# Reshaped loads of x, a class without mirrored rows, and constant tables moved between engines, in a Fourier-mixing + MLP-Mixer kernel

## The chip, the cores and the metric

The kernel runs on one core of one Trainium2 chip. The metric is the device time of one execution, in microseconds (us), lower is better. "Span" is the time of the one execution that was profiled, from its first to its last instruction; it is 1.7 to 3.0 us shorter than the time measured for the same execution.

Engine names in the profile: PE is TensorE's matrix products, PEld its weight loads, DVE is VectorE, ACT is ScalarE, POOL is GpSimd, SP is SyncE. L315 is line 315 of that kernel's source; lines shift by a few between kernels.

## The reference

```python
x: (8, 3008, 256)      # batch, sequence, features
x = np.fft.fft(np.fft.fft(x, axis=1), axis=2).real          # Fourier mixing
h = np.maximum(x.transpose(0, 2, 1) @ w_tok1, 0) @ w_tok2   # token MLP: 3008 -> 256 -> 3008
u = x + h.transpose(0, 2, 1)
out = u + np.maximum(u @ w_ch1, 0) @ w_ch2                  # channel MLP: 256 -> 1536 -> 256
```

The sequence length is factored as 3008 = 47 x 64. A real Fourier transform has mirror symmetry, so the kernel needs, beside each row of x, the row mirrored around the middle of the sequence.

## The kernel before

All loads go out through GpSimd's queue. `load_x` brings a batch into two tiles: `xp`, the rows in order, as two copies of 47 partitions, and `xm`, the mirrored rows, as gathers of 94 rows (two gathers of 8 rows of x at a time, and a third gather of one row for the class r = 0, which are the rows whose number is a multiple of 64).

```python
KR = 2 * NQ            # 94
def load_x(b, between=None):
    xp = xin.tile([KR, NR, D], FP16, tag="xp", name="xp")
    xm = xin.tile([KR, NR, D], FP16, tag="xm", name="xm")
    for i in range(2):
        nc.gpsimd.dma_start(
            out=xp[i * NQ:(i + 1) * NQ, :, :],
            in_=dram(x_t, (b * S + 16 * i) * D, [[64 * D, NQ], [1, NR * D]]))
    ...
    xmf = xm[:].rearrange("p t d -> p (t d)")
    for k in range(2):
        gather(xmf[:, 8 * D * k:8 * D * (k + 1)], x8, ix8[0:KR, b, k:k + 1])
    gather(xmf[:, 16 * D:17 * D], x1, ix1[0:KR, b:b + 1])
    return xp, xm
```

Behind batch 0 in the same queue come the weights: w_tok1 in order (`w1p`) and mirrored (`w1m`), w_tok2 (`w2s`), then the channel weights. Meanwhile VectorE and ScalarE build the sine tables: the small tables of the first stage (`cs`, `t1n`, `t1a`, `t1b`), of the feature stage (`td0`, `td1`), and the large third-stage tables (`tp`, `tq`). VectorE works out the reduced angles, ScalarE takes the sine.

Then come the pieces that decide when the steady stage can begin:

```python
def turned(src, sgn):      # transposes on PE, evicted by ScalarE -> tt
    ...
def carried(tts, dst):     # token weights carried through the third stage
    for g2 in range(NG // 2):
        ph = ps_mm("ph")
        for k in range(2):
            ...
            nc.tensor.matmul(o, lhsT=tts[0][:, g, :], rhs=w1p[:, g, :], ...)             # L313
            nc.tensor.matmul(o, lhsT=tts[1][:, g, :], rhs=w1m[:, NG - 1 - g, :], ...)    # L315
        copy(...)
...
tts_p = turned(tp, 1.0)
tts_q = turned(tq, -1.0)
take(fold(0, nc.vector), 4)    # sums and differences of xp and xm -> eo, on VectorE
...
own = front(0)                 # the Fourier stages of batch 0: pz products first
take(own, 4)
carried(tts_p, hp)
take(own, 4)
carried(tts_q, hq)
...                            # rest of front(0), then the channel MLP (mm1, mm2) for all batches
```

`front(b)` starts with products `pz` of `eo` with `t1n`, evicted to `z`. In the program of PE the first four groups of `pz` stand ahead of the carried products (and in its trace they start at 28.8 us, the carried products at 33.7), so these need the turned tables, w1p, w1m, and the `pz` products ahead of them.

## Time and profile before

| before | |
|---|---|
| time, median of the first 3 runs | 698.62 us (697.92 to 698.90) |
| span of the profiled execution | 695.8 us |
| PE busy | 655.8 us (94%) |
| first carried product that needs w1m | 35.5 us |
| first product of the channel MLP (`pc`) | 57.26 us |

The first two lines of the page give the totals:

```profile
span 695.8 us, 12517 instructions
...
PE 655.8 (94%) x5342; PEld 460.3 (66%) x5342; DVE 336.5 (48%) x621; ACT 318.0 (46%) x604; POOL 222.6 (32%) x180
```

Those 94% are an average over a start in which PE is mostly idle and a long stage in which it never is. The windows view shows it. Each line is a stretch of time, its length, then the busy time (and number of instructions) of each engine, the granted clock of PE, the DMA share and GB/s:

```profile
core 0: us, PE busy (x) PEld busy (x) DVE busy (x) ACT busy (x) POOL busy (x), PEclk, DMA share, GB/s
0.00:20.00 20.00, 1.46 (x12) 1.30 (x13) 15.46 (x61) 5.64 (x9) 11.59 (x20) 1.00 0.96 117
20.00:35.00 15.00, 6.42 (x39) 3.55 (x39) 8.96 (x20) 8.59 (x14) 3.83 (x5) 0.77 1.33 182
35.00:50.00 15.00, 11.70 (x97) 9.38 (x97) 7.99 (x14) 9.80 (x17) 6.16 (x5) 0.84 1.06 171
150.00:600.00 450.00, 450.00 (x3735) 317.63 (x3733) 203.92 (x353) 210.46 (x413) 161.83 (x120) 1.00 0.25 55
```

From 150 to 600 us PE is busy in 450.00 of 450 us, so there is no idle time of PE that a faster engine or load could fill. What this change can win lies in the first 60 us. The chain of waits (start, length, what) says what the start is waiting for:

```profile
10.99 0.67 POOL w1p L144
11.66 23.83 DMA w1m<-in_moe_w_tok_dram
...
35.53 0.37 PE ph L315
```

One load, w1m, takes 23.8 us from its issue, and PE's first product with it starts at once when it lands. The DMA view (tiles, queue, kind, number, KB each, median us from issue to landing) shows that everything near the gathers is slow, but not the direct copies of x:

```profile
DMA packets 50583, 44.03 MB, mean 63 GB/s; under 512 B 18144, under 2 KB 47504, under 8 KB 49776
...
xp<-in_x_dram POOLq DMA_DIRECT2D x16, 399.5 KB, 6.2
...
w2s<-in_moe_w_tok_dram POOLq DMA_DIRECT2D x1, 1504.0 KB, 31.0
...
w1m<-in_moe_w_tok_dram POOLq DMA_DIRECT2D x1, 384.0 KB, 23.8
...
xm<-in_x_dram,ix_77 POOLq DMA_INDIRECT x16, 21.2
```

Of the 16 completion events of that w1m, 12 had come by 24.9 us, when the gathers had landed (24.5 and 25.1 us); the other four came at 35.0 to 35.5 us. The Trainium skill ("DMA: Bandwidth & Descriptors", section "Why a DMA increments its semaphore by 16 and not by 1") says that each engine posts its own increment after its own share of the data. Four of sixteen engines were thus late with their share. The completion events of the two gathers of 94 rows ahead show which: of the first gather's 16 events, 14 came by 8.6 us and two only at 23.9 and 24.5; of the second's, 12 came by 9.4 us and four at 24.6 to 25.1. So the rows of the first gather sat on two engines, the second added two more, and the loads behind them came late on just those four.

### The profile page before, as it was taken

The page shows a single profiled execution, that of the slowest core. Times are in us where ns is not written, and L with a number is a line of the kernel's source. Part 1 is how long each engine was busy: PE and PEld are TensorE (multiplying, and loading weights), DVE is VectorE, ACT ScalarE, POOL GpSimd, SP SyncE. Part 2 cuts the span into 40 slices and gives each one's busy share as a digit, 9 for nine tenths or more (in the row PEclk, how much of TensorE's full clock was granted, in tenths as well). Part 3 has the DMA queues.
Part 4 walks back from the last instruction along what each step waited for, and adds up shares of the span by engine and source line. Part 5 has one row for each costly group of instructions (what it writes and reads, how often), then busy time and mean ns, then how long its engine had stood idle before and what let it go on. Part 6 is the DMA issues. An engine that isn't in the chain of part 4 may idle for free.

```text
span 695.8 us, 12517 instructions
## 1 busy us (share of the span) xinstructions
PE 655.8 (94%) x5342; PEld 460.3 (66%) x5342; DVE 336.5 (48%) x621; ACT 318.0 (46%) x604; POOL 222.6 (32%) x180
## 2 busy tenths in 40 slices
PE   0479999999999999999999999999999999999996
PEld 0265667666766677666776677667776677666665
DVE  8547863653445433654345533554335533453341
ACT  2556553445443555344543554344453454434342
POOL 6230209909902393208810294206700000000000
PEclk9889999999999999999999999999999999999999
DMA  8992341441432126212431116311111211211222
GB/s 111 178 174 41 77 78 33 78 90 47 80 78 61 28 53 117 50 31 58 82 75 46 43 31 116 72 31 40 50 31 31 57 33 31 54 38 35 54 61 57
DMA packets 50583, 44.03 MB, mean 63 GB/s; under 512 B 18144, under 2 KB 47504, under 8 KB 49776
## 3 DMA queue, kind: packets, MB, share of 16 engines
q0 software_dynamic: 24928, 18.60, 17.6%
q1 hardware_dynamic: 25600, 24.65, 13.9%
q8 instruction: 41, 0.67, 0.4%
q14 instruction: 14, 0.11, 0.1%
HBM read 37.06 MB, written 24.64 MB: 89 GB/s over the span
## 4 chain that ended last, share of the span: by engine, by line
PE 91%; DMA 3%; DVE 3%; ACT 1%; POOL 1%; issue 1%; ACTq 0%; DVEq 0%; POOLq 0%
PE po L481 36%; PE pc L460 34%; PE pu L436 6%; DMA w1m<-in_moe_w_tok_dram 3%; PE py L419 2%; PE py L421 2%; PE po L484 2%; PE po L486 2%; PE pw L389 1%; PE pz L366 1%; PE pw L390 1%; ACT w2p L324 1%; PE ph L315 0%; DVE ut L444 0%; PE ph L313 0%
## 5 line engine op out<-in xcount | busy, mean ns | idle before, releaser
L460 PE MATMUL pc<-ut,wc1p 128*128 128x512 f16 x576 | 140.7, 379 | 2.3 <-DVE c_681 L85 1.2
L460 PE MATMUL pc<-ut,wc1m 128*128 128x512 f16 (+1 forms) x576 | 135.1, 370 | 0.0
L491 ACT ACTIVATE osb<-po 128x512 f32<-128x512 f32 x88 | 52.6, 598 | 113.2 <-PE po L486 113.2
L460 PEld LDWEIGHTS <-wc1m 128*128 128x128 f16 x576 | 54.0, 98 | 51.6 <-issue 0.4
L460 PEld LDWEIGHTS <-wc1p 128*128 128x128 f16 x576 | 52.3, 98 | 52.7 <-issue 4.4
L444 DVE TENSOR_TENSOR ut<-pu,yt 128x512 f16<-128x512 f32 (+1 forms) x96 | 61.6, 674 | 52.0 <-PE pu L436 52.0
L347 POOL TENSOR_TENSOR xd<-xp,xm 94x1024 f16<-94x1024 f16 (+1 forms) x24 | 53.7, 2238 | 98.8 <-DMA xm<-in_x_dram,ix_77 98.8
L349 POOL TENSOR_TENSOR eo<-xp 94x512 f16<-94x512 f16 (+1 forms) x24 | 29.1, 1211 | 111.0 <-PE pz L378 109.4
L348 POOL TENSOR_TENSOR xp<-xp,xm 94x1024 f16<-94x1024 f16 (+1 forms) x24 | 53.7, 2237 | 1.9
L436 PE MATMUL pu<-w2p,uu 128*128 128x512 f16 (+1 forms) x192 | 50.1, 375 | 0.0
L486 PE MATMUL po<-anti,ut 128*128 128x128 f16 x192 | 41.8, 218 | 0.0
L484 PE MATMUL po<-ident,ut 128*128 128x128 f16 x192 | 41.7, 217 | 0.0
L324 ACT ACTIVATE w<-pw 128x258 f16<-128x258 f32 x90 | 30.5, 385 | 23.3 <-PE pw L390 23.1
L423 ACT ACTIVATE yt<-py 128x512 f16<-128x512 f32 x48 | 26.6, 597 | 21.1 <-PE py L421 16.7
L322 DVE CAST z<-pz 128x480 f16<-128x480 f32 (+1 forms) x36 | 22.4, 691 | 24.4 <-PE pz L366 15.9
L353 POOL TENSOR_TENSOR eo<-xd 94x508 f16<-94x508 f16 (+1 forms) x24 | 29.0, 1207 | 0.0
L324 ACT ACTIVATE z<-pz 128x480 f16<-128x480 f32 (+1 forms) x28 | 18.3, 670 | 20.1 <-PE pz L366 19.9
L123 POOL DMA_INDIRECT xm<-in_x_dram,ix_77 x16 | 24.3, 1518 | 4.8 <-issue 4.8
L419 PE MATMUL py<-tp,w 128*128 128x128 f16 x192 | 24.7, 219 | 0.7 <-DVE ut L444 0.7
L389 PE MATMUL pw<-td_161,z 128*128 128x258 f16 x96 | 21.8, 274 | 2.9 <-ACT w L324 1.5
L436 PEld LDWEIGHTS <-uu 128*128 128x128 f16 x192 | 16.4, 97 | 9.1 <-issue 0.2
L131 POOL DMA_DIRECT2D xp<-in_x_dram x16 | 9.2, 582 | 39.8 <-DVE eo L351 39.6
(404 smaller groups left out, 1274.5 us busy)
## 6 DMA issues: line engine op xcount, KB each, us to landing
out_dram<-osb SPq DMA_DIRECT2D x88, 256.0 KB, 3.4
xp<-in_x_dram POOLq DMA_DIRECT2D x16, 399.5 KB, 6.2
out_dram<-osb SPq DMA_DIRECT2D x8, 192.0 KB, 3.1
w2s<-in_moe_w_tok_dram POOLq DMA_DIRECT2D x1, 1504.0 KB, 31.0
w1p<-in_moe_w_tok_dram POOLq DMA_DIRECT2D x2, 384.0 KB, 20.5
wc_129<-in_moe_w_ch_dram POOLq DMA_DIRECT2D x1, 768.0 KB, 23.5
w1m<-in_moe_w_tok_dram POOLq DMA_DIRECT2D x1, 384.0 KB, 23.8
wc1p<-in_moe_w_ch_dram POOLq DMA_DIRECT2D x1, 384.0 KB, 19.6
```

What stands on the lines that cost most here:

```text
L324: nc.scalar.activation(out=out_, in_=in_, func=AFT.Copy)
L347: eng.tensor_tensor(out=xd[:, t, :], in0=xp[:, t, :], in1=rv, op=AT.subtract)
L348: eng.tensor_tensor(out=xp[:, t, :], in0=xp[:, t, :], in1=rv, op=AT.add)
L349: eng.tensor_tensor(out=eo[:, t, 1:129], in0=xp[:, t, 1:129], in1=xp[:, t, 255:127:-1], op=AT.add)
L419: nc.tensor.matmul(o, lhsT=w[:, g, h:h + P], rhs=tp[:, g, :], start=True, stop=False)
L436: nc.tensor.matmul(pu[:, 0:n], lhsT=uu[:, th, v, o:o + P], rhs=w2p[:, th, f0:f0 + n], start=(th == 0), stop=(th == 1))
L444: nc.vector.tensor_tensor(out=ut[:, h, f0:f0 + n], in0=pu[:, 0:n], in1=y, op=AT.add)
L460: nc.tensor.matmul(pc[:, 0:n], lhsT=wc[:, h, ct * P:(ct + 1) * P], rhs=ut[:, h, f0:f0 + n], start=(h == 0), stop=(h == 1))
L481: nc.tensor.matmul(po[0:n, o:o + D], lhsT=c1[:, ct, ks * P:ks * P + n], rhs=wc2[:, ct, minus:minus + D], start=(ct == 0), stop=False)
L484: nc.tensor.matmul(po[0:n, o:o + P], lhsT=ut[:, 0, f0:f0 + n], rhs=ident[:], start=False, stop=False)
L486: nc.tensor.matmul(po[0:n, o + P:o + D], lhsT=ut[:, 1, f0:f0 + n], rhs=anti[:], start=False, stop=True)
L491: nc.scalar.activation(out=osb[:, ks - 1:ks + 1, minus:minus + D], in_=src, func=AFT.Copy)
```

## The change

Its intent: spread the loads of x over more DMA engines by giving them piece sizes that divide well; drop the third gather, by treating the class r = 0 without mirrored rows; make the large third-stage tables first on VectorE, and the small tables on GpSimd beside it (so the first loads of the channel weights, which GpSimd issues too, move behind these tables). Its core (full of small moves of code, cut at "..."):

```diff
+KG = 96
...
-    ts(ix8[:], ix8f[:], rowi[:], AT.add)
-    ...                                    # ix1: indices of the third gather
+    ts(ix8[:], ix8f[:], rowi[:], AT.add, 0.0, AT.max)
...
-        xm = xin.tile([KR, NR, D], FP16, tag="xm", name="xm")
+        xm = xin.tile([KG, NR - 1, D], FP16, tag="xm", name="xm")
         for i in range(2):
-            nc.gpsimd.dma_start(out=xp[i * NQ:(i + 1) * NQ, :, :], ...)
+            for q, n in ((0, 32), (32, NQ - 32)):
+                p0 = i * NQ + q
+                nc.gpsimd.dma_start(out=xp[p0:p0 + n, :, :], ...)
...
-            gather(xmf[:, 8 * D * k:8 * D * (k + 1)], x8, ix8[0:KR, b, k:k + 1])
-        gather(xmf[:, 16 * D:17 * D], x1, ix1[0:KR, b:b + 1])
+            gather(xmf[:, 8 * D * k:8 * D * (k + 1)], x8, ix8[0:KG, b, k:k + 1])
...
-    for t in (tp, tq):
-        nc.vector.memset(t[:], 0.0)
+    for t in (tp, tq):                      # zeroed by ScalarE instead
+        for i in range(2):
+            ...nc.scalar.activation(out=t[...], in_=kb[...], func=AFT.Copy, scale=0.0)
...
+    # third-stage tables tp, tq first, on VectorE; then all small tables:
+    pl = nc.gpsimd
+    ts(mask0[:], xicol[:], -1.0, AT.mult, 1.0, AT.add, eng=pl)
+    ...                                     # cs, t1n, t1b, td0, td1: the same with eng=pl
...
-        for t0, t1 in ((13, 17), (9, 13), (5, 9), (0, 5)):
+        for t0, t1 in ((13, 17), (9, 13), (5, 9), (1, 5)):
...
+            if t0 == 1:
+                t = slice(0, t1)
+                eng.tensor_copy(out=xd[:, 0, :], in_=xp[:, 0, :])
...
-                copy(half and b > 0, zo[:, :, :, t0:t0 + 5],
+                copy(half, zo[:, :, :, t0:t0 + 5],
...
-            nc.tensor.matmul(pz[:, 0:24], lhsT=eo[0:NQ, 0, c], rhs=t1a[0:NQ, :], ...)
+            nc.tensor.matmul(pz[:, 0:24], lhsT=eo[0:NQ, 0, c], rhs=t1n[0:NQ, half, 0, :], ...)
+            if half:
+                nc.tensor.matmul(pz[0:1, 0:24], lhsT=eo[0:NQ, 0, P:P + 1],
+                                 rhs=t1n[0:NQ, 0, 0, :], start=True, stop=True)
```

## The prediction

> **What bounds it now.** The busy table gives TensorE 655.8 of 695.8 us; in the windows from 150 to 600 us it is always busy. It idles at the start: 18.5 us of the first 20, 8.6 of the next 15, 3.3 of the next 15; the end costs 5.8 us. There the chain of waits runs through one 23.8 us wait for the last mirrored piece of w_tok1 (w1m); then TensorE starts the carried-weight products (line 315) at 35.5 us. Ready before: turned tables at 26.1 us (timeline, ScalarE), first fold at 33.9.
>
> **Why that DMA is late.** The mirrored gathers (94 rows) take 15 to 17 us. Packet records (144 to 154 us) show about 11 of 4 KB per us, 0.322 us each: some 3.6 DMA engines for two gathers; 47 x 0.322 = 15.1 us. The Trainium skill ("DMA: Bandwidth & Descriptors", "Why a DMA increments its semaphore by 16 and not by 1") says that the engine count is the largest up to 16 dividing the row counts: 2 for 94, 16 for 96. The trace agrees. Loads behind share these engines: of the last w1m's completion events, 12 came by 24.9 us and four at 35.0 to 35.5.
>
> **What the change does.** With 96 rows, 16 engines move 6 packets each, an estimated 1.9 us per gather. Fold data is there at 11-12 us instead of 25, w1m at 23-25 instead of 35.5, w2s near 32 instead of 43.4. One 1.5 us gather goes; two more xp issues (0.58 each) come. xp already spread (94 packets in about 5 us), so splitting it gains nothing. None of it is on the path in the steady stage.
>
> VectorE begins the third-stage tables at about 5 us instead of 12.4; ScalarE zeroes first and pays a second table load (1.28 us), so its sines of tp/tq end near 13-14 us instead of 19.8. GpSimd makes the small tables after five w1/w2 issues, from about 12.5 us: 20-odd operations of 0.2 to 0.7 us, estimated 6 us alone. They overlap the first fold (9.1 us on VectorE), whose operations have two SBUF inputs; the Trainium skill ("SBUF — State Buffer", "Who interferes with whom") says that such instructions and GpSimd reads exclude each other. No stretch of this trace shows that pair, so I allow 3 to 6 us more. ScalarE runs in order, so its copies of the turned tables (6.3 us) wait for the last small sines, at 18-24 us. The turned tables, not w1m, become the last input of the carried products: start at about 28 us (25 to 32) instead of 35.5.
>
> Added: eight one-row matmuls, an estimated 0.5 us.
>
> **Predicted time.** 698.6 - 7.5 + 0.5 = 691.6 us; 8 in 10: 688.0 to 696.0. Chances: faster by over 2% 0.05, within 2% 0.94, slower 0.01.
>
> **What would show each step.** Gathers landing within 4 us of issue, also late in the run; first fold starting at 11-12 us; ScalarE's copies of the turned tables (tt) preceded by a wait for GpSimd's tables; the first carried product at 25 to 32 us, not released by a DMA; windows from 150 us on unchanged.
>
> **What would make it wrong.** GpSimd tables starved by the fold, so that the turned tables come no earlier than 33 us (gain near zero); or hardly disturbed, so that carried products start by 24 us (gain 11 us). A 2% gain (14 us) would need a start by 21 us, before w1m can land.

## The result, and the profile after

The changed kernel took 692.51 us (median of 4 runs, 691.42 to 693.89) beside 698.27 us for the kernel before (4 runs, 697.39 to 698.90). Ratios here are the mean time of one kernel's fast runs over that of the other's in the same rounds, so they are not quite the ratio of the medians; this one is 0.9919, with a 95% interval of 0.9894 to 0.9945. It is a gain of 0.8%, within the 2% that counts as the same. Here are the page's totals and the same windows:

```profile
span 692.1 us, 12556 instructions
...
PE 656.3 (95%) x5350; PEld 461.4 (67%) x5350; DVE 326.5 (47%) x597; ACT 321.3 (46%) x607; POOL 216.8 (31%) x214
```

```profile
core 0: us, PE busy (x) PEld busy (x) DVE busy (x) ACT busy (x) POOL busy (x), PEclk, DMA share, GB/s
0.00:20.00 20.00, 1.46 (x12) 1.30 (x13) 18.02 (x52) 9.91 (x12) 17.41 (x33) 1.00 1.04 160
20.00:35.00 15.00, 9.92 (x62) 6.64 (x62) 3.42 (x7) 9.42 (x17) 11.07 (x19) 1.00 1.15 204
35.00:50.00 15.00, 12.36 (x135) 10.75 (x134) 8.27 (x21) 9.26 (x18) 0.99 (x1) 0.89 0.81 161
150.00:600.00 450.00, 450.00 (x3732) 317.99 (x3731) 199.74 (x351) 209.52 (x411) 147.79 (x127) 1.00 0.24 54
```

The steady stage is as before. From 0 to 35 us VectorE, ScalarE and GpSimd all do more, and PE still does nearly nothing in the first 20 us. The DMA view:

```profile
DMA packets 34201, 43.74 MB, mean 63 GB/s; under 512 B 2480, under 2 KB 31088, under 8 KB 33392
...
xp<-in_x_dram POOLq DMA_DIRECT2D x16, 272.0 KB, 5.9
xp<-in_x_dram POOLq DMA_DIRECT2D x16, 127.5 KB, 6.0
...
w2s<-in_moe_w_tok_dram POOLq DMA_DIRECT2D x1, 1504.0 KB, 17.4
...
w1m<-in_moe_w_tok_dram POOLq DMA_DIRECT2D x1, 384.0 KB, 11.3
...
xm<-in_x_dram,ix_76 POOLq DMA_INDIRECT x16, 8.0
```

The gathers land in 8.0 us instead of 21.2, w1m in 11.3 instead of 23.8; w1m is there at 21.1 us and the first fold starts at 11.1 instead of 24.6. All 16 completion events of the first gather now come together, at 9.8 to 10.3 us. The pieces of xp take as long as the whole copies did. The chain of waits no longer has a load in it:

```profile
22.22 0.74 POOL gr L223
...
22.98 0.31 ACT td_201 L227
23.30 0.20 ACT td_202 L227
23.49 1.41 ACT tt L296 x2
...
28.19 1.01 PE pr L300 x2
29.20 0.81 PE pz L368 x10
...
31.32 0.21 PE ph L312
31.53 0.21 PE ph L314
```

Read it from the top: GpSimd's last small table (`gr`), its two sines on ScalarE, then ScalarE's copies of the turned tables, which come behind those sines in ScalarE's program order, then PE's products, then the carried products at 31 us. From issue to landing the loads got 12 to 14 us faster; the first carried product with w1m comes only 4.2 us sooner (35.53 to 31.32). Note which executions were profiled: that of the kernel before took 697.54 us, near its fastest, and that of the changed kernel 693.89 us, its slowest, so the two spans differ by only 3.7 us where the medians differ by 5.8.

**A ruler for all that follows.** In every one of the 14 profiles, the span is the start of the first channel-MLP product (`pc`) plus a constant: 638.5 to 638.6 us in the three of kernels that keep the third gather (before, e1, e2), and 639.1 to 639.3 us in the other eleven, of kernels that have the r = 0 class. So everything except 0.7 us is decided before `pc` starts, and 0.7 us is what the r = 0 class costs after it.

| kernel | first w1p product | first `pc` | span | span - `pc` |
|---|---|---|---|---|
| before | 33.74 | 57.26 | 695.8 | 638.5 |
| after | 31.11 | 52.91 | 692.1 | 639.2 |
| after, profiled again (e11) | 30.10 | 50.32 | 689.5 | 639.2 |
| e1 | 26.78 | 47.72 | 686.3 | 638.6 |
| e10 | 27.77 | 48.71 | 687.9 | 639.2 |
| e7 | 23.91 | 45.48 | 684.7 | 639.2 |
| e9 | 24.55 | 46.61 | 685.8 | 639.2 |
| e12 | 21.86 | 43.26 | 682.5 | 639.2 |

### The profile page after: what moved, and what is told of

The parts are those of the page before. It is cut to its first block, busy times and chain, and to the rows that moved or that the text cites. A ratio compares the mean times of both kernels' runs of the same rounds, so it can differ in the third digit from the quotient of the medians.

```text
span 692.1 us, 12556 instructions
## 1 busy us (share of the span) xinstructions
PE 656.3 (95%) x5350; PEld 461.4 (67%) x5350; DVE 326.5 (47%) x597; ACT 321.3 (46%) x607; POOL 216.8 (31%) x214
## 4 chain that ended last, share of the span: by engine, by line
PE 92%; DVE 3%; POOL 2%; ACT 2%; issue 1%; ACTq 0%; DVEq 0%; POOLq 0%
PE po L487 37%; PE pc L466 34%; PE pu L442 6%; PE py L425 2%; PE pz L368 2%; PE py L427 2%; PE po L490 2%; PE po L492 2%; PE pw L395 1%; PE pw L396 1%; ACT w2p L323 1%; DVE ut L450 1%; PE ph L312 0%; PE ph L314 0%; ACT tt L296 0%
## 5 line engine op out<-in xcount | busy, mean ns | idle before, releaser
L346 POOL TENSOR_TENSOR xd<-xp,xm 94x1024 f16<-94x1024 f16 x24 | 50.8, 2117 | 33.7 <-DMA xm<-in_x_dram,ix_76 33.7
L347 POOL TENSOR_TENSOR xp<-xp,xm 94x1024 f16<-94x1024 f16 x24 | 50.8, 2117 | 1.9
L323 ACT ACTIVATE w<-pw 128x258 f16<-128x258 f32 x90 | 30.5, 385 | 23.4 <-PE pw L396 23.3
L321 DVE CAST z<-pz 128x480 f16<-128x480 f32 (+1 forms) x39 | 24.5, 677 | 34.2 <-PE pz L368 26.2
L429 ACT ACTIVATE yt<-py 128x512 f16<-128x512 f32 x48 | 26.6, 597 | 21.1 <-PE py L427 16.7
L127 POOL DMA_DIRECT2D xp<-in_x_dram x32 | 17.2, 562 | 38.6 <-DVE eo L353 38.3
L323 ACT ACTIVATE z<-pz 128x480 f16<-128x480 f32 (+1 forms) x25 | 16.7, 672 | 15.8 <-PE pz L368 15.6
L490 PEld LDWEIGHTS <-ut 128*128 128x128 f16 x192 | 18.9, 98 | 2.7
## 6 DMA issues: line engine op xcount, KB each, us to landing
w1m<-in_moe_w_tok_dram POOLq DMA_DIRECT2D x1, 384.0 KB, 11.3
```

The lines of the kernel that those rows point to most:

```text
L323: nc.scalar.activation(out=out_, in_=in_, func=AFT.Copy)
L346: eng.tensor_tensor(out=xd[:, t, :], in0=xp[:, t, :], in1=rv, op=AT.subtract)
L347: eng.tensor_tensor(out=xp[:, t, :], in0=xp[:, t, :], in1=rv, op=AT.add)
L490: nc.tensor.matmul(po[0:n, o:o + P], lhsT=ut[:, 0, f0:f0 + n], rhs=ident[:], start=False, stop=False)
```

## The experiments

My theory after the result: the whole gain is the 96-row gathers; the split of xp is worth nothing; and the small tables on GpSimd became the last input of the carried products, which gave part of the gain back. Rivals: the split spreads the x copies and is part of the gain; the dropped third gather is; the fold or the loads, and not GpSimd's tables, hold the carried products. Twelve kernels ran, in four groups; all gave the right result. The time of the kernel before was 698.47, 698.26, 697.85 and 698.80 us in the four groups (9 to 11 runs each).

### e1: the kernel before, with gathers of 96 rows

```diff
+KG = 96
-    ts(ix8[:], ix8f[:], rowi[:], AT.add)
+    ts(ix8[:], ix8f[:], rowi[:], AT.add, 0.0, AT.max)     # and ix1 the same
-        xm = xin.tile([KR, NR, D], FP16, tag="xm", name="xm")
+        xm = xin.tile([KG, NR, D], FP16, tag="xm", name="xm")
-            gather(..., x8, ix8[0:KR, b, k:k + 1])        # and the third gather
+            gather(..., x8, ix8[0:KG, b, k:k + 1])
```

> The kernel before with 96-row instead of 94-row gathers (all three), nothing else. Gather theory (94 rows sit on 2 DMA engines each and block the weight loads behind them on those engines): last w1m lands by about 20 us instead of 35.5; VectorE's tables and ScalarE's turned tables stay as they were (done at 26.1 us), fold from 18 to 27 us, so the first carried product starts at about 27 us, 4 us earlier than in the changed kernel; time 688 to 690 us. Table theory (the gain comes from third-stage tables being first and the small ones on GpSimd): no gain without them, 697 to 699 us. Split theory (xp in 32+15 is what spreads the loads): 697 to 699 us as well.

Measured: 689.36 us (688.05 to 689.55, 4 runs), ratio 0.9869 (0.9854 to 0.9884). This part alone gains 9.1 us, more than the whole change. w1m landed at 21.3 us, and up to 60 us no product that makes the carried weights waits for a load. PE's timeline (start, length, line, operation, tiles, shapes) has the first carried product here:

```profile
26.78 0.27 PE L314 MATMUL ph<-w1p,tt 128*128 128x256 f16 x1
```

Nothing else of the change is needed for the gain. (The clamp of the index to 0 or more belongs to the edit: the two padding rows would otherwise point ahead of the start of x for batch 0.) The number of packets under 512 B falls from 18144 to 2352 by this edit alone, so those small packets belong to the 94-row gathers: 658 for each of the 24, which is 14 x 47, as if each of the 14 engines without rows had got 47 of them (that reading is not shown). They are not what holds the loads up: in the kernel before, of the 2106 four-byte packets from 3 to 26 us 1762 had started by 11 us, at a median of 9 ns each, while the 4 KB packets of the two large gathers ran from 7 to 24.5 us, about 12 per us and 0.324 us each (12 x 0.324: some 4 engines at a time).

### e2: the kernel before, with xp in pieces of 32 + 15

```diff
-            nc.gpsimd.dma_start(out=xp[i * NQ:(i + 1) * NQ, :, :], ...)
+            for q, n in ((0, 32), (32, NQ - 32)):
+                p0 = i * NQ + q
+                nc.gpsimd.dma_start(out=xp[p0:p0 + n, :, :], ...)
```

> The kernel before with xp loaded in pieces of 32 and 15 partitions, nothing else. Gather theory: gathers still on 2 engines, w1m at 35 to 37 us, time 697 to 699.5 us (two more issues of 0.58 us before the gathers may cost up to 1 us). Split theory: gathers or weights land several us earlier, time under 695 us. It also shows which part of the change removed the 4-byte packets (16608 before, 944 after): if they belong to the 47-row copies they go to about 1000 here, if to the 94-row gathers they stay.

Measured: 699.36 us (698.44 to 699.86, 5 runs), ratio 1.0011 (0.9997 to 1.0024). The split gains nothing; the interval just touches 1. The pieces land in 5.7 and 6.0 us, the whole copies in 6.2, and the small packets stay (18400). The rival that the 47-row copies were badly spread falls.

### e3: the changed kernel, with gathers of 94 rows again

```diff
-KG = 96
+KG = 94
```

> The changed kernel with its gathers put back to 94 rows, all else kept. Gather theory: w1m lands at 33 to 36 us again and is again what the carried products wait for; time 696 to 699 us, as before. Table theory: the gain stays, 691 to 694 us.

Measured: 700.62 us (700.21 to 701.19, 5 runs), ratio 1.0029 (1.0015 to 1.0043): slower than the kernel before. I had expected no more than 699, so the rest of the change costs 1 to 2 us more than I thought. In its chain of waits, the load is back:

```profile
11.39 27.18 DMA w1m<-in_moe_w_tok_dram
...
38.61 0.37 PE ph L314
```

The gathers land in 20.0 us and w1m in 27.2. From here to the changed kernel (692.51) is 8.1 us for one constant, close to the 9.1 of e1: the gathers' worth is about the same in either surrounding.

### e4: the changed kernel, with xp in two copies of 47 again

```diff
-            for q, n in ((0, 32), (32, NQ - 32)):
-                ...
+            nc.gpsimd.dma_start(out=xp[i * NQ:(i + 1) * NQ, :, :], ...)
```

> The changed kernel with xp again in two copies of 47 partitions. Gather theory with 'splitting gains nothing': 691 to 693 us, perhaps 0.5 to 1 us faster through two issues fewer before the gathers. Split theory: 694 to 698 us.

Measured: 691.44 us (691.26 to 691.69, 4 runs), ratio 0.9898 (0.9883 to 0.9913). Two issues fewer stand ahead of the gathers, and the first carried product starts at 29.9 us instead of 31.1. The split is not a gain in this surrounding either; whether it loses is not settled here, since the changed kernel's own runs come in two groups (e11), and e4's four lie with the faster one.

### e5: the changed kernel, with VectorE's first fold held back until GpSimd's tables are done

```diff
     tts_q = turned(tq, -1.0)
+    held = const.tile([P, 4], FP16, tag="held", name="held")
+    nc.vector.tensor_copy(out=held[:], in_=td1[:, 0:4])
     take(fold(0, nc.vector), 4)
```

> The changed kernel with VectorE's first fold held back until GpSimd's last small table is written (a small VectorE copy that reads it). Exclusion theory (GpSimd's small tables are slow because the fold's two-input instructions on VectorE and GpSimd's reads of SBUF exclude each other): from its first small table to the last remainder (gr), which took 11.6 us in the changed kernel, GpSimd now takes about 6 us; the turned tables are done near 24 us although the fold ends only near 27 us; 689 to 692 us. Slow-GpSimd theory (its operations take 0.4 to 1.0 us whatever VectorE does): still about 11 us, the fold ends near 34 us, 694 to 698 us.

Measured: 691.96 us (691.50 to 692.30, 4 runs), ratio 0.9912 (0.9896 to 0.9928). The time is that of the changed kernel, for the fold is now the late one: the carried products start at 27.7 us, 2.4 to 3.4 us sooner, but some 15 of them run at half rate and PE then waits 0.7 us for a copy of hp, so that the last carried product starts at 36.7 us, as in e11 (the changed kernel profiled again). What this run measures is GpSimd without VectorE's fold beside it. GpSimd's timeline in the changed kernel:

```profile
11.35 0.51 POOL L88 TENSOR_SCALAR mask_172<-xicol 128x1 f32<-128x1 f32 x1
...
13.24 1.01 POOL L86 TENSOR_SCALAR m_178<-krow,qcol 94x48 f32<-94x48 f32 x1
...
22.22 0.73 POOL L223 TENSOR_TENSOR gr<-gv,md 128x258 f32<-128x258 f32 x1
```

and the same three instructions with the fold held:

```profile
11.32 0.22 POOL L88 TENSOR_SCALAR mask<-xicol 128x1 f32<-128x1 f32 x1
...
12.33 0.42 POOL L86 TENSOR_SCALAR m<-krow,qcol 94x48 f32<-94x48 f32 x1
...
18.34 0.73 POOL L223 TENSOR_TENSOR gr<-gv,md 128x258 f32<-128x258 f32 x1
```

The stretch from the first of them to the end of the last is 11.60 us beside the fold and 7.75 us without it: 3.9 us of interference. Other runs repeat both numbers: 11.6 in e11 and 11.8 in e4, where the fold runs beside it, and 7.8 in e3, where the fold starts only at 23.8 us. Single small instructions double here (0.22 to 0.51, 0.42 to 1.01) but differ from run to run (0.22 and 0.50 for the same two in e11); the last one starts after the changed kernel's fold ended (20.6 us) and is the same in both. The Trainium skill ("SBUF — State Buffer", section "Who interferes with whom") says that a VectorE instruction with two SBUF inputs contends with a GpSimd instruction that reads SBUF; this pair of runs agrees and puts a size on it. VectorE hardly pays: its fold takes 9.5 us beside GpSimd, 9.0 alone.

### e6: the changed kernel, with the turned tables ahead of the small tables in program order

```diff
+    def turned(src, sgn): ...          # moved up
+    tts_p = turned(tp, 1.0)
+    tts_q = turned(tq, -1.0)
     pl = nc.gpsimd
     ...                                # small tables, as in the changed kernel
-    tts_p = turned(tp, 1.0)
-    tts_q = turned(tq, -1.0)
     take(fold(0, nc.vector), 4)
```

> The changed kernel with the turned tables made (transposes, products, ScalarE's copies) before the small tables, so that ScalarE's copies no longer stand behind the small sines. If these copies are what the carried products wait for, as I claim: copies from 13.4 to about 20 us, carried products after the first front products at 22 to 25 us instead of 31; 684 to 687 us. If something else holds them (fold, w1m, front products): 690 us or more.

Measured: 686.64 us (685.42 to 688.75, 5 runs), ratio 0.9838 (0.9818 to 0.9857). The work is the same to the instruction, and only its order differs. ScalarE's first copies of the turned tables and its last sines in the changed kernel:

```profile
22.98 0.31 ACT L227 ACTIVATE td_201<-gr 128x129 f16<-128x129 f32 x1 [5.95 <-POOL gr L223]
...
23.40 1.49 ACT L296 ACTIVATE tt<-pt 128x768 f16<-128x768 f16 x2
```

and the same two, with PE's first carried product, in e6:

```profile
13.41 1.51 ACT L257 ACTIVATE tt<-pt 128x768 f16<-128x768 f16 x2
...
24.56 0.51 ACT L227 ACTIVATE td<-gr 128x129 f16<-128x129 f32 x2 [4.43 <-POOL gr L223]
...
22.82 0.41 PE L315 MATMUL ph<-w1p,tt 128*128 128x256 f16 x1
```

ScalarE copies the turned tables from 13.4 to 19.8 us instead of 23.4 to 29.9, and the carried products start at 22.8. This shows what the chain of the changed kernel only suggested: program order on ScalarE behind GpSimd's late tables cost 5 to 6 us (686.64 against 691.78 and 692.51). PE now waits 2.23 us for GpSimd's `t1n` instead.

### e7: the changed kernel, with the small tables on VectorE

```diff
-    pl = nc.gpsimd
+    pl = nc.vector
```

> The changed kernel with the small tables on VectorE again (after the third-stage tables, before the fold), all else kept. If putting them on GpSimd cost time: VectorE makes them in about 5 us (11 to 16 us), ScalarE's turned copies run 16 to 23 us, carried products at 24 to 26 us; 685 to 688 us, faster than both kernels. If GpSimd's part was a gain: 692 us or more.

Measured: 686.22 us (685.34 to 687.76, 5 runs), ratio 0.9830 (0.9813 to 0.9847). On VectorE the small tables take 5.9 us (11.05 to 16.9), and the fold waits for them until 17.0; still the carried products start at 23.9 us. Moving the tables to the idle engine was the part that lost, given the order of ScalarE's program: e6 leaves them on GpSimd, changes that order, and is as fast. The rest of that move (third-stage tables first, ScalarE doing the zeroing) gains: e7 against e10 below is 686.22 against 690.20.

### e8: e6, with the carried products ahead of the first products of batch 0

```diff
     own = front(0)
-    take(own, 4)
     carried(tts_p, hp)
-    take(own, 4)
     carried(tts_q, hq)
-    take(own, 3)
+    take(own, 11)
```

> As the run with the turned tables first, and also the carried products ahead of the first front products. Nothing but w1m (19 us) and the turned copies (20 us) is then ahead of them: start at 20 to 21 us; 681 to 686 us, 1 to 3 us under the run with the turned tables alone. If the loads of w2, wc1 or wc2, or the fold, then bind: the same as that run.

Measured: 688.45 us (687.19 to 690.35, 4 runs), ratio 0.9869 (0.9848 to 0.9890). My expectation of a further gain failed; it is slower than e6. The carried products do start earlier, at 19.9 us, but PE then waits 1.93 us for w1m, which lands at 22.2 (the 19 us of my expectation was the landing of w1p), and then starts them 0.21 us apart until 25.7; from 26.4 on it starts them 0.11 us apart. In e6 the spacing falls to 0.11 us after 25.2. The last carried product starts 2.0 us sooner than in e6 (29.9 against 31.9), but what had been mixed in with the carried products now comes after them alone:

```profile
29.99 0.80 PE L371 MATMUL pz<-t1n,eo 94*128 94x96 f16 x15
```

With the waits for the copies of z these `pz` products last until 33.9 us, when the next stage (`pw`) starts; in e6 that is at 32.0. So, as far as this profile shows, it is this order that loses, and the half speed takes a part of the early start. That spacing pointed to PE's clock, which e11 shows.

### e11: the changed kernel again

```diff
+# the changed kernel again, nothing edited
```

> The changed kernel again, on a chip with the runs above: 691 to 694 us. Its two earlier pairs of runs (691.5 and 693.7) differ by 2 us; in its profile (693.9) TensorE's clock was slow until 33.8 us. If that is the difference, a profile at 691.5 shows the clock full from about 28 to 30 us, and one at 693.5 from about 33 us.

Measured: 691.78 us (691.43 to 693.87, 6 runs), ratio 0.9922 (0.9907 to 0.9938). The six runs fall in two groups: 691.43, 691.44, 691.70, 691.86 and 693.67, 693.87. So did the first four: 691.42, 691.56 and 693.46, 693.89. The profile shown above is of the last, this one of 691.43. Its chain of waits at the same place:

```profile
30.27 0.11 PE ph L312
30.38 0.11 PE ph L314
```

The same products stand 0.11 us apart here and 0.21 in the other profile. The clock records in the trace (the full-rate and half-rate stretches, from which the PEclk column is made) begin with full rate at 27.1 us here and at 33.8 us there; the PEclk column prints 1.00 before the first record, so it does not show this, but the spacing does. The Trainium skill ("TensorE: Matmul & The Clock Gate", Part 1) says that PE runs at half rate by default, at full rate after a busy window of 3.4 us, and that the window runs free of the kernel's start, so that the point of change varies from run to run. The trace agrees: the half-rate and full-rate stretches at the start of these profiles are 3.4, 6.8, 10.2 or 13.7 us long, that is 1 to 4 times 3.41, and two runs of one kernel differ in them. The two spans differ by 2.6 us (692.1 against 689.5), and 1.5 us of that lies between the first carried product with w1m and `pc` (21.6 against 20.1). That the other slow runs have the same cause is likely but not shown, as only these two have a profile.

### e9: first-stage tables on VectorE, turned tables next, feature-stage tables on GpSimd

```diff
-    pl = nc.gpsimd
+    pl = nc.vector
     ...                                # cs, t1n, t1b
+    tts_p = turned(tp, 1.0)            # as in e6, but here
+    tts_q = turned(tq, -1.0)
+    pl = nc.gpsimd
     ...                                # md, td0, td1
```

> What the runs so far point to: third-stage tables first and then the small first-stage tables on VectorE (about 3.5 us there), then the turned tables, and only the feature tables (td, not needed until about 30 us) on GpSimd with their sines behind ScalarE's turned copies. Copies from 13.7 to 20 us, fold from about 14.5 to 24 us, carried products from about 22 us; 683 to 686 us, a little under the two runs at 686. If the slow TensorE clock at the start or the fold binds instead, it stays at 685 to 688.

Measured: 687.60 us (686.83 to 688.28, 5 runs), ratio 0.9852 (0.9838 to 0.9865): above the range that I expected, a miss. The carried products start at 24.6 us. PE's timeline shows in brackets what it waited for just before them:

```profile
24.19 0.56 PE L372 MATMUL pz<-t1n,eo 94*128 94x96 f16 x5 [2.65 <-DVE z L325]
24.55 0.41 PE L316 MATMUL ph<-w1p,tt 128*128 128x256 f16 x1
```

The fourth set of `pz` products needs a free PSUM buffer, and the copy that would free it sits on VectorE behind the whole fold. It is the edit of `copy(half and b > 0, ...)` to `copy(half, ...)`, the smallest line of the change.

### e10: e1 with the r = 0 class of the change

```diff
-        gather(xmf[:, 16 * D:17 * D], x1, ix1[0:KG, b:b + 1])
...                                     # fold and front for r = 0 as in the changed kernel
```

> The kernel before with 96-row gathers and the r = 0 class without mirrored rows, tables untouched. The one-row matmuls (an estimated 0.5 us in all) and the third gather saved about cancel: 688.5 to 690 us, as with 96-row gathers alone. Then the 2 to 3 us by which the changed kernel is slower than 96-row gathers alone are the move of the tables. If it is 691 us or more, the r = 0 class costs them instead.

Measured: 690.20 us (688.68 to 691.14, 5 runs), ratio 0.9888 (0.9873 to 0.9904), between the two ranges expected, against 0.9869 for e1 in another group: a loss of about 1 us, with intervals that overlap. By the ruler, about 0.6 us of it is the longer steady stage (8 more matmuls). The profiled span had another 1.0 us at the start, where some of VectorE's table instructions took longer than in e1 (two of them 0.72 us instead of 0.30); why is not shown. Dropping the third gather does not gain.

### e12: e9, with batch 0's copies of z back on ScalarE

```diff
-                copy(half, zo[:, :, :, t0:t0 + 5],
+                copy(half and b > 0, zo[:, :, :, t0:t0 + 5],
```

> The mixed kernel with the first batch's copies of the front products (z) all on ScalarE, as in the kernel before. In the mixed run these products waited 2.65 us for a copy on VectorE that stood behind the fold (which ended at 23.5 us), so the carried products began at 24.5 us instead of 22. With the copies on ScalarE, free from 20.3 us, they should begin at 21.5 to 22.5 us; 684.5 to 686.5 us if the clock lets them run at full speed. If the slow clock (until 27.7 us in the mixed run) takes the gain back: 687 us or more, as there.

Measured: 684.39 us (683.73 to 684.77, 5 runs), ratio 0.9793 (0.9777 to 0.9810). The wait of e9 is gone:

```profile
21.08 0.98 PE L372 MATMUL pz<-t1n,eo 94*128 94x96 f16 x10 [0.89 <-DVE eo L357]
21.86 0.41 PE L316 MATMUL ph<-w1p,tt 128*128 128x256 f16 x1
```

It beats both kernels: 14.4 us under the kernel before of the same group, and 7 to 9 us under the changed one, by the medians or by the ratios. Whether it is faster than before by over 2% is unclear by the interval. PE still runs the first carried products at half rate here; the full rate begins at 23.9 us.

### What the parts are worth

Following the ratios along one path of kernels, times 698 us (estimates; the steps compare different groups on different chips, each with its own runs of the kernel before, and each is good to about 1 us):

| step | ratio | us |
|---|---|---|
| before to e1: 96-row gathers | 1 to 0.9869 | -9.1 |
| e1 to e10: r = 0 class | 0.9869 to 0.9888 | +1.3 |
| e10 to e7: third-stage tables first, zeroing on ScalarE, split, z copies | 0.9888 to 0.9830 | -4.0 |
| e7 to after (e11): small tables on GpSimd | 0.9830 to 0.9922 | +6.4 |
| sum | 0.9922 | -5.4 |

## Why the prediction was right, point by point

- **The total.** Predicted 691.6 us (688.0 to 696.0), measured 692.51. The mechanism held, but the closeness of the number is partly luck: the earlier start of the carried products was put at 7.5 us and was 4.2 us in one profile and 5.3 in the other, and in the second the way from there to `pc` was 1.6 us shorter (21.7 us before, 20.1 in e11) with PE at full rate, which the prediction did not have in its sum.
- **What bounds it, and why: right.** w1m was the wait, and the gathers ahead of it the reason. e1 removes the cause alone and gains 9.1 us; e3 brings it back alone and loses 8.1. The rule that the prediction took from the Trainium skill ("DMA: Bandwidth & Descriptors", same section as above), 2 engines for 94 rows and 16 for 96, agrees with the gathers' 21.2 us falling to 8.0. The many small packets, which vanish with the same edit, are no rival: the completion events (14 early and two late for the first gather, all 16 together with 96 rows) show the number of engines, and five in six of the small packets around the first gathers had started by 11 us (e1).
- **The split gains nothing: right** (e2, e4).
- **The turned tables become the last input, behind GpSimd's tables on ScalarE: right.** The last small sines came at 23.0 us (predicted 18 to 24), the first carried product at 31.1 (predicted 28, range 25 to 32), not released by a load. e6 takes the order away and gains 5 to 6 us.
- **VectorE and GpSimd excluding each other: right in kind.** GpSimd's tables: 6 us alone was estimated, 7.75 was measured (e5); 3 to 6 us of interference was allowed, 3.9 was measured.
- **Nothing changes in the steady stage: nearly right.** PE is busy 450.00 of 450 us in both. The eight one-row matmuls were put at 0.5 us; the ruler gives 0.6 to 0.7.
- **Mis-sized: the loads.** w1m was expected at 23 to 25 us and came at 21.1, w2s near 32 and came at 28.0. The statement "gathers landing within 4 us of issue" failed: the median is 8.0, probably because each batch's gathers are queued behind its own copies of xp, which take 5.9. Neither was on the path after the change, so the total did not feel them.
- **Mis-sized: the gain at the carried products.** 7.5 us was expected; the first w1m product came 4.2 us earlier in one profile (35.53 to 31.32) and 5.3 in the other (to 30.21). The last small sines started at 23.0 us, late in the range of 18 to 24, and after the last copy of the turned tables (29.9 us) came another 1.2 us of `pz` products and a copy of z, for which the sum had no term.
- **Left out: PE's clock.** The prediction took PE's products as having one speed. In the kernel before, the first dozen carried products ran at half rate (until 38.2 us), and in the changed kernel the end of the half rate lies at 27.1 us in one run and at 33.8 in another, whose spans differ by 2.6 us.

## What to carry to other kernels

When a load on the critical path takes far longer than its size asks for, look at what was issued ahead of it in the same queue: here two rows of padding on a gather, from 94 to 96, were worth more than the whole change that contained them. Before moving small work to an idle engine, ask which in-order engine consumes its results and what stands behind them in that engine's program; here the "free" tables on GpSimd cost 6 us through ScalarE's queue. When the steady stage is saturated, measure each variant by when that stage starts: that one time, plus a constant, gave every span.

## What the Trainium skill lacked or had wrong

- "DMA: Bandwidth & Descriptors" (how k, the number of engines, is chosen) was confirmed in its effect (94 rows 21.2 us, 96 rows 8.0), and its exception for direct copies too: two copies of 47 partitions land in 6.2 us, about as fast as pieces of 32 and 15 (5.7 and 6.0 in e2). It does not say that a badly dividing gather also brings many small packets (18144 under 512 B before, 2352 in e1: 658 a gather), nor what it does to the loads behind it: a 384 KB load took 23.8 us, 12 of its completions by 24.9 us and four more than 10 us later.
- "SBUF — State Buffer" (who interferes with whom) gives the rule but no size for a stream of small GpSimd instructions beside two-input VectorE ones: 11.6 us against 7.75 (11.6 and 11.8 in e11 and e4, 7.8 in e3), while VectorE lost about 0.5 us of 9.
- "TensorE: Matmul & The Clock Gate" puts the ramp at under 1% of a typical kernel. That agrees (2.6 of 692 us), but such a difference is as large as many changes one wants to judge, and it makes two groups of runs of one kernel. What no page says is that the granted-clock column of a profile can print 1.00 while the products still stand at the half-rate spacing (0.21 us against 0.11), as it does here before the first clock record.
- "ScalarE: Activation LUTs" (what ACT_TABLE_LOAD costs) gives some 1283 ns for the load, which agrees (1.28 us), and about 1380 ns of drain on top, of which the trace of the changed kernel shows nothing: the zeroing copy before it ended at 8.69 us, the load started at 8.69, ended at 9.97, and the first sine started at 9.99.
